# Two small products of a linear attention laid out in halves and quarters of the matrix array

## The chip, the cores and the metric

The kernel runs on one core of a Trainium2 chip. The metric is the device time of one execution in microseconds (us), less is better. The core has a matrix engine (PE, with PEld for its weight loads), a vector engine (DVE), a scalar engine (ACT), GpSimd (POOL), a queue of transfers on SyncE (SP), and DMA engines. PE reads its operands from the on-chip memory and writes into accumulation banks (PSUM), which DVE and ACT empty.

## The reference

Linear attention over 4 batches of 8 heads with 576 rows of 64, then two feed-forward blocks over all 2304 rows (model width 512, inner width 1536). All is float32.

```python
q_s = softmax(q, axis=-1)            # over the 64 features of a row
k_s = softmax(k, axis=2)             # over the 576 rows
kv  = einsum('bhsd,bhse->bhde', k_s, v)      # 64 x 64 for each head
x   = einsum('bhsd,bhde->bhse', q_s, kv)     # then heads side by side: 2304 x 512
x   = (silu(x @ w_gate) * (x @ w_val)) @ moe_w_out
out = ((x @ w_a) * (x @ w_b)) @ moe2_w_out
```

## The kernel before

**Tiles.** The attention is worked in 16 units: 4 batches (b) by 4 pairs of heads (g). A unit holds two heads side by side in the 128 columns or partitions (HG = 2, D = 64), and its 576 rows as four slices of 128 (R = 4) and a rest of 64. The names in a unit are `kx`, `kb` (turned maxima of k, and their spread over the partitions), `kv` (k^T v of both heads), `ks` (sums and reciprocals), `kvbd` (a 128 by 128 matrix with the two scaled 64 by 64 blocks on its diagonal, zero elsewhere), `qt` and `ql` (q turned, main part and rest), `xt` and `xl` (x turned, main part and rest). Buffers of the first two batches are called `ut`; those of the third and fourth `ua`, `uc` and `uq`.

**k^T v (lines 726 to 750).** Five products per unit add up in one PSUM tile of 128 by 130: weights are 128 columns of k (two heads), the moving operand is 130 columns of v (two heads of 64, each with a column of ones that gives the sum of k). The result also holds the two products of one head's k with the other head's v; they are left unread. DVE or ACT scales the two wanted 64 by 64 blocks into `kvbd`.

**x (lines 790 to 800).** One product per unit with `kvbd` as weights and 512 moving columns. For the first batch the result goes straight into the on-chip operand `xhl` of the first feed-forward block. For the other three batches ACT copies it to the buffer `xs` and issues one transfer of 256 KB to a buffer in device memory, from which a later block reads it.

**Feed-forward blocks.** Every float32 weight is converted into a high and a low part by a chain of ACT, DVE and POOL instructions (`convert`, lines 404 to 441), and each product is three reduced-precision products of these parts. The first feed-forward block runs over the batches 0 and 1 as f = 0 to 11 (`u` at line 857, `acc` at line 884); the other work of that block and the second one uses sub-products `p`, `q`, `o` (lines 1136, 1220, 1247 to 1257). The units of batch 1 stand among the products of batch 0 in the first block, those of batches 2 and 3 among those of batch 1.

**What sets the order.** Every instruction is an entry of a plan (`add`), with an engine, an assumed cost, what it reads and writes, and a due time that is worked out backwards or given. `Plan.order` simulates the engines with these costs and picks, per engine, the ready entry that is due first; entries with a second engine (`other`) go where they would end earlier; PSUM banks are given out in the same pass. `Plan.search` repeats that 160 times, shifts a few due times at random each time, and keeps the shortest plan. The instructions are then written out in that order, and each engine runs its own list strictly in that order; an instruction waits until its operands and its buffer are there. So the assumed costs and the seed of the random shifts (line 220) set the order of all engines.

Of the kernel before, what the change touches and what calls it, by code (L numbers as in the profile page):

```python
# [9 lines left out]
F32 = mybir.dt.float32  # L10
# [21 lines left out]
class Plan:  # L32
# [184 lines left out]
    def search(self):  # L217

        self.prepare()
        rng, best = random.Random(0), None  # L220
        for n in range(self.ROUNDS):
            kept = self.due
            if best:
                self.due = [d + rng.uniform(-3, 3) if rng.random() < 0.03 else d for d in kept]
            try:
                found = self.order()
            except RuntimeError:
                self.due = kept
# [16 lines left out]
def kernel(  # L245
# [24 lines left out]
    nc = tc.nc  # L270
# [78 lines left out]
    WHOLE = ("a0", "xraw")  # L349
    AHEAD = 3  # L350
    TOP = 122880.0
    LEAST = 2.0 ** -15

    NP = NF // 2
# [171 lines left out]
    def attend(b, g, xhl, due):  # L526
# [30 lines left out]
        def kx():  # L557
            return col(A, a0, m).rearrange("p (r e) -> p r e", r=R)
# [16 lines left out]
        def vx():  # L575
            return vg()[:, 0:G, :].rearrange("p (h r) d -> p h r d", h=HG)
# [18 lines left out]
        def small(shape, tag):  # L595
            return Buf(hp, shape, F32, (tag + "0", tag + "1"), f"{tag}{u}")

        def psum(shape, name, tag=None):
            if b == 0 and tag:
                return Buf(pg, shape, F32, (tag,), f"{name}{u}")  # L600
            return Buf(pg, shape, F32, AT_BANKS[b], f"{name}{u}")
# [121 lines left out]
            row(ql, m, G, [*QRL, (st, "maxl")], QL)  # L723


        pk, ks = psum([P, HG, D1], "kv"), small([P, 2, HG], "ks")

        def kv():
            for r in range(R):
                nc.tensor.matmul(pk(), lhsT=kx()[:, r, :], rhs=vx()[:, :, r, :], start=(r == 0), stop=False)  # L730
            nc.tensor.matmul(pk(), lhsT=kl(), rhs=vg()[:, G:G + 1, :].to_broadcast([P, HG, D1]),
                             start=False, stop=True)

        add("tensor", 1.3, kv, [K_, KL, *VS, VL, (C, "ones")], [pk])
        add("vector", 0.16, lambda: nc.vector.tensor_scalar(
            out=ks()[:, 0, :], in0=pk()[:, :, D], scalar1=EPS, scalar2=None, op0=ALU.add), [pk], [ks])
        add("vector", 0.16, lambda: nc.vector.reciprocal(out=ks()[:, 1, :], in_=ks()[:, 0, :]), [ks], [ks])
        for h in range(HG):
            o = rest_cols(h)

            def scale(h=h, o=o):
                nc.vector.tensor_scalar(out=kvbd()[o, o], in0=pk()[o, h, 0:D], scalar1=ks()[o, 1, h:h + 1],
                                        scalar2=None, op0=ALU.mult)

            def scale_too(h=h, o=o):
                nc.scalar.mul(out=kvbd()[o, o], in_=pk()[o, h, 0:D], mul=ks()[o, 1, h:h + 1])
# [33 lines left out]
        def turn_rest():  # L780
# [6 lines left out]
        add("scalar", act_us(SL), lambda: nc.scalar.copy(out=qT()[:, SM:S], in_=pl()), [pl], [QTL])  # L787


        px, py = psum([P, SM], "xt", f"acc{g}"), Buf(pg, [P, SL], F32, AT_BANKS[max(b, 1)], f"xl{u}")  # L790
        add("tensor", 0.95, lambda: nc.tensor.matmul(  # L791
            px(), lhsT=kvbd(), rhs=qT()[:, 0:SM], start=True, stop=True), [QT, *BDS], [px], due=due)
        if xhl is not None:
            split(lambda: xhl()[:, 0, g, :], lambda: xhl()[:, 1, g, :], px, SM,
                  (xhl, (0, g)), (xhl, (1, g)), px, psum=True)
# [233 lines left out]
    def parts(s):  # L1029
# [6 lines left out]
        for q, (t, h) in enumerate(((0, 0), (0, 1), (1, 0), (1, 1))):  # L1036
            i = blocks[t]
            pieces = [(i, 0, width, 0)] if i < B else [(i - 1, width, SM - width, 0), (i, 0, B * SL, SM - width)]
            for src, at, size, to in pieces:
                last_x[:] = [dma(lambda q=q, h=h, src=src, at=at, size=size, to=to: nc.sync.dma_start(  # L1040
                    out=RAW[q][1]().rearrange("p (c n) -> p c n", c=2)[:, :, to:to + size],
                    in_=xd[l][src]()[:, 2 * h:2 * h + 2, at:at + size]),
                    P * 2 * size * 4, [(xd[l][src], (2 * h + c, 0)) for c in range(2)] if s == 0 else [xd[l][src]],
                    [(RAW[q][0][0], (RAW[q][0][1], to))], after=[*last_x, *(() if s or t == 0 else pair_buf["after"])])]

        def keys(q):
# [328 lines left out]
```

## Time and profile before

| | us |
|---|---|
| median of 3 runs (lowest, highest) | 946.86 (946.19, 947.77) |
| the profiled execution, its own time | 947.02 |
| its span in the trace | 945.2 |
| PE busy | 913.9 (97%) |
| DVE busy | 641.7 (68%) |
| ACT busy | 519.2 (55%) |

The profile comes from one execution. A busy time of PE contains the way through the array of each product, which overlaps with the next product; so products that stand back to back show a longer duration than the distance of their starts. In the chain of waits a step counts only the time until the next step begins, which is the time that the product really takes from the span. A float32 product appears as two passes, each with its own weight load (x2 for one product).

### The profile page before, as it was taken

To read this page: it belongs to the slowest core of one execution; us is meant where nothing else is said; L and a number is where in the kernel's file an instruction comes from. 1 tells how busy PE (TensorE), PEld (TensorE's weight loads), DVE (VectorE), ACT (ScalarE), POOL (GpSimd) and SP (SyncE) were. 2 spreads that over 40 slices of the span, in tenths; PEclk is the share of its full clock that TensorE was granted. 3 is DMA by queue.
4 is the path that set the end of the run, shared out by engine and by line. 5 is a ranking of instruction groups with operands and counts; after the bars stand their busy time and mean duration, and the time that the engine had idled before them with its cause. 6 is when DMAs were issued, how large, how long until landed. Compare 5 with 4: busy or idle time off the path is not lost.

```text
span 945.2 us, 12797 instructions
## 1 busy us (share of the span) xinstructions
PE 913.9 (97%) x4400; PEld 755.7 (80%) x4400; DVE 641.7 (68%) x1025; ACT 519.2 (55%) x1020; POOL 331.9 (35%) x323
## 2 busy tenths in 40 slices
PE   5699999999999999999999999999999999999998
PEld 4477777788887888888888888888888888888886
DVE  6899996544376887877778665775786444564444
ACT  4798876878675665455464456443644453333310
POOL 6534221112053322434455542432565113342210
PEclk9889999999999999999999999999999999999999
DMA  9858765464327545355322653422213210110003
GB/s 263 271 199 267 233 230 190 121 191 131 90 89 233 156 143 153 123 163 156 112 90 71 214 174 121 133 89 89 68 50 123 86 45 23 45 45 23 23 1 112
DMA packets 108153, 121.43 MB, mean 128 GB/s; under 512 B 31928, under 2 KB 83896, under 8 KB 107960
## 3 DMA queue, kind: packets, MB, share of 16 engines
q1 hardware_dynamic: 102424, 116.55, 39.8%
q10 hardware_dynamic: 5664, 4.07, 1.4%
q8 instruction: 35, 0.57, 0.3%
q14 instruction: 30, 0.25, 0.1%
HBM read 88.60 MB, written 31.98 MB: 128 GB/s over the span
## 4 chain that ended last, share of the span: by engine, by line
PE 80%; DVE 8%; DMA 6%; ACT 3%; issue 2%; SPq 1%; POOL 0%; DVEq 0%; ACTq 0%
PE p L1136 34%; PE o L1247 15%; PE u L857 9%; PE q L1220 7%; PE o L1249 6%; PE acc L884 5%; PE o L1257 2%; DVE l2w L324 1%; PE kv L730 1%; DMA wr<-in_moe_w_gate_dram 1%; PE xt L791 1%; DVE sums L324 1%; DMA wr<-in_moe_w_out_dram 1%; DMA wf<-a 1%; DMA raww<-wf 1%
## 5 line engine op out<-in xcount | busy, mean ns | idle before, releaser
L1136 PE MATMUL p<-l2w,l2w 128*128 128x512 f32 x1512 | 353.1, 390 | 1.3 <-DVE temps L324 1.1
L1136 PEld LDWEIGHTS p<-l2w,l2w 128*128 128x128 f32 x1512 | 283.1, 188 | 61.7 <-DVE temps L324 2.4
L857 PE MATMUL u<-xhl,w 128*128 128x512 f32 x552 | 143.9, 408 | 5.0 <-DVE w L324 4.7
L331 ACT CAST l2w<-raww 128x512 fp32r<-128x512 f32 x144 | 88.1, 621 | 79.7 <-PE p L1136 39.9
L324 POOL TENSOR_TENSOR l2w<-raww,l2w 128x512 fp32r<-128x512 f32 x68 | 97.0, 1431 | 97.9 <-ACT l2w L331 97.8
L857 PEld LDWEIGHTS u<-xhl,w 128*128 128x128 f32 x552 | 102.2, 192 | 31.8 <-DVE w L324 6.8
L324 DVE TENSOR_TENSOR sums<-o,sums 128x512 f32<-128x512 f32 x120 | 82.4, 689 | 53.4 <-PE o L1247 39.9
L324 DVE TENSOR_TENSOR temps<-p,temps 128x512 f32<-128x512 f32 x90 | 62.1, 690 | 66.4 <-PE p L1136 65.2
L1247 PE MATMUL o<-l2w,hp 128*128 128x512 f32 x288 | 82.3, 394 | 0.3 <-DVE sums L324 0.2
L1148 ACT COPY temps<-p 128x512 f32<-128x512 f32 x72 | 42.4, 588 | 68.3 <-PE p L1136 68.2
L324 DVE TENSOR_TENSOR l2w<-raww,l2w 128x512 fp32r<-128x512 f32 x76 | 55.6, 742 | 26.6 <-ACT l2w L331 26.5
L884 PE MATMUL acc<-h,w 128*128 128x512 f32 x288 | 73.6, 399 | 0.0
L1220 PE MATMUL q<-rest,l2w 128*128 128x256 f32 x432 | 65.4, 283 | 0.0
L1247 PEld LDWEIGHTS o<-l2w,hp 128*128 128x128 f32 x288 | 53.4, 188 | 12.9 <-DVE sums L324 1.8
L884 PEld LDWEIGHTS acc<-h,w 128*128 128x128 f32 x288 | 52.9, 188 | 11.9
L1220 PEld LDWEIGHTS q<-rest,l2w 128*128 128x128 f32 x432 | 58.6, 192 | 0.9
L1247 PE MATMUL o<-l2w 128*128 128x512 f32 x192 | 54.5, 392 | 0.0
L496 POOL TENSOR_TENSOR latewr<-latewr 128x512 uint32<-128x512 uint32 x17 | 23.9, 1410 | 63.5 <-DVE latewr L491 47.9
L1247 PE MATMUL o<-l2w,l2w 128*128 128x512 f32 x168 | 44.6, 390 | 0.0
L324 POOL TENSOR_TENSOR raww<-raww,spare 128x512 f32<-128x512 f32 x15 | 20.1, 1339 | 69.2 <-DVE l2w L324 63.8
L1249 PE MATMUL o<-hp,l2w 128*128 128x512 f32 x144 | 41.9, 399 | 1.6 <-DVE sums L324 1.6
L1247 PEld LDWEIGHTS o<-l2w 128*128 128x128 f32 x192 | 36.0, 188 | 8.2
(197 smaller groups left out, 1483.5 us busy)
## 6 DMA issues: line engine op xcount, KB each, us to landing
raww<-wf SPq DMA_DIRECT2D x36, 512.0 KB, 4.2
raww<-wf SPq DMA_DIRECT2D x36, 256.0 KB, 3.6
wf<-latewr SPq DMA_DIRECT2D x36, 256.0 KB, 3.4
wf<-a SPq DMA_DIRECT2D x16, 384.0 KB, 2.8
latewr<-in_moe_w_a_dram SPq DMA_DIRECT2D x24, 256.0 KB, 3.0
latewr<-in_moe_w_b_dram SPq DMA_DIRECT2D x24, 256.0 KB, 3.6
latewr<-in_moe_w_out_dram SPq DMA_DIRECT2D x12, 512.0 KB, 5.0
wr<-in_moe_w_gate_dram SPq DMA_DIRECT2D x22, 256.0 KB, 3.1
```

Source lines behind the costliest of these rows:

```text
L324: engine.tensor_tensor(out=out(), in0=x(), in1=y(), op=op)
L331: add("scalar", act_us(n), lambda: nc.scalar.copy(out=hi(), in_=src()), src_keys, [hi_key])
L496: engine.tensor_tensor(out=u32(), in0=u32(), in1=r()[..., 0], op=ALU.add)
L730: nc.tensor.matmul(pk(), lhsT=kx()[:, r, :], rhs=vx()[:, :, r, :], start=(r == 0), stop=False)
L857: nc.tensor.matmul(ps()[:, 0:n], lhsT=wv[:, c, :], rhs=x()[:, xs, c, 0:n], start=(a == 0 and c == 0), stop=(a == 2 and c == KD - 1))
L884: nc.tensor.matmul(ps()[:, 0:n], lhsT=w()[:, 4 + ws, o * P:(o + 1) * P], rhs=h()[:, hs, 0:n], start=begin, stop=end)
L1136: nc.tensor.matmul(ps()[:, 0:width], lhsT=wv(o)[:, m, ws, c, :], rhs=ops_x[o][xs][1]().rearrange("p (c n) -> p c n", c=2)[:, c, 0:width], ...
L1148: add("scalar", act_us(n), lambda: nc.scalar.copy(out=to[1]()[:, 0:n], in_=ps()[:, 0:n]), [ps], [to[0]], due=main["at"] + main["soon"])
L1220: nc.tensor.matmul(ps[m]()[:, 0:256], lhsT=wv(o)[:, m, ws, c % 2, :], rhs=rest_x[xs][1]().rearrange("p (c n) -> p c n", c=KD)[:, c, :], st ...
L1247: nc.tensor.matmul(ps(), lhsT=lhs(i, hs), rhs=outs_w[i][1]()[:, ws * 512:(ws + 1) * 512], **ends)
L1249: nc.tensor.matmul(ps()[:, 0:width], lhsT=outs_w[i][1]()[:, ws * 512 + r * P:ws * 512 + (r + 1) * P], rhs=hs2[i][t][1]()[:, hs * 512:hs * ...
L1257: nc.tensor.matmul(ps()[:, o * 256:(o + 1) * 256], lhsT=outs_w[i][1]()[:, ws * 512 + at:ws * 512 + at + P], rhs=rest_h[1]()[:, (2 * i + hs ...
```

## The change

The change does four things. k^T v of a unit is ten products of 64 by 65 instead of five of 128 by 130: for each slice of rows first head 0, with its 64 weight columns in the left column half of the array (`tile_position=(0, 0)`, results in the PSUM partitions 0 to 63), then head 1 in the right half (`(0, 64)`, partitions 64 to 127). The products of one head with the other head's v are no longer computed. x of batches 1 to 3 is four products of 64 by 64 weights with 256 moving columns each, in the four quarters of the array (`tile_position=(h * D, t * D)`, head h and half t of the columns); the two of one head go into one PSUM tile, the second head into another; ACT makes two copies of 256 columns, and issues two transfers of 128 KB. Batch 0 keeps its single product. The plan's assumed costs become 0.8 for k^T v (1.3 before) and 0.27 for each pair of products of x (0.95 before for the one product), and the seed becomes 2.

```diff
-        rng, best = random.Random(0), None
+        rng, best = random.Random(2), None
...
+    XT = 0.27
+    KV = 0.8
...
-        pk, ks = psum([P, HG, D1], "kv"), small([P, 2, HG], "ks")
+        pk, ks = psum([P, D1], "kv"), small([P, 2], "ks")
 
         def kv():
-            for r in range(R):
-                nc.tensor.matmul(pk(), lhsT=kx()[:, r, :], rhs=vx()[:, :, r, :], start=(r == 0), stop=False)
-            nc.tensor.matmul(pk(), lhsT=kl(), rhs=vg()[:, G:G + 1, :].to_broadcast([P, HG, D1]),
-                             start=False, stop=True)
-
-        add("tensor", 1.3, kv, [K_, KL, *VS, VL, (C, "ones")], [pk])
+            for r in range(R + 1):
+                for h in range(HG):
+                    lhs, rhs = (kx()[:, r, rest_cols(h)], vx()[:, h, r, :]) if r < R else (kl()[:, rest_cols(h)], vg()[:, G, :])
+                    nc.tensor.matmul(pk()[rest(h), :], lhsT=lhs, rhs=rhs, start=r == 0, stop=r == R,
+                                     tile_position=(0, h * D))
+
+        add("tensor", KV, kv, [K_, KL, *VS, VL, (C, "ones")], [pk])
...
-        px, py = psum([P, SM], "xt", f"acc{g}"), Buf(pg, [P, SL], F32, AT_BANKS[max(b, 1)], f"xl{u}")
-        add("tensor", 0.95, lambda: nc.tensor.matmul(
-            px(), lhsT=kvbd(), rhs=qT()[:, 0:SM], start=True, stop=True), [QT, *BDS], [px], due=due)
...
-            ob = Buf(op, [P, 512], F32, ("ob0", "ob1"), f"xs{u}")
-            add("scalar", act_us(SM), lambda: nc.scalar.copy(out=ob(), in_=px()), [px], [ob])
-            dma(lambda: nc.scalar.dma_start(out=xd[0][b]()[:, g, :], in_=ob()), P * SM * 4,
-                [ob], [(xd[0][b], (g, 0))], queue="scalar")
+            ob, half = Buf(op, [P, 512], F32, ("ob0", "ob1"), f"xs{u}"), SM // 2
+            for h in range(HG):
+                ph = psum([P, half], f"xt{h}_")
+
+                def run(h=h, ph=ph):
+                    for t in range(2):
+                        nc.tensor.matmul(ph()[t * D:(t + 1) * D, :], lhsT=kvbd()[rest_cols(h), rest_cols(h)],
+                                         rhs=qT()[rest_cols(h), t * half:(t + 1) * half], start=True, stop=True,
+                                         tile_position=(h * D, t * D))
+
+                add("tensor", XT, run, [QT, *BDS], [ph], due=due)
+                add("scalar", act_us(half), lambda h=h, ph=ph: nc.scalar.copy(
+                    out=ob()[:, h * half:(h + 1) * half], in_=ph()), [ph], [(ob, h)])
+            for t in range(2):
+                dma(lambda t=t: nc.scalar.dma_start(
+                    out=xd[0][b]()[:, g, t * half:(t + 1) * half].rearrange("(h e) n -> e h n", h=HG),
+                    in_=ob()[t * D:(t + 1) * D, :].rearrange("e (h n) -> e h n", h=HG)), P * SM * 2,
+                    [ob], [(xd[0][b], (g, t))], queue="scalar")
```

The new costs and the new seed move instructions on every engine. Line numbers of the changed kernel are 2 to 18 higher: 734 is k^T v (730 and 731 before), 807 is x of the later batches (791 before), 875 and 902 are `u` and `acc` (857 and 884 before).

On PE, at the second unit of batch 2, among the products of the first feed-forward block; before:

```order
L884 MATMUL acc_1_1727<-h_1_0_1675,w_0_329 128x512 x3
L730 MATMUL kv_1741<-uc_1549,ua_1557 128x130 x4
L731 MATMUL kv_1741<-uc_1549,ua_1557 128x130
L884 MATMUL acc_2_1755<-h_1_0_1675,w_0_329 128x512 x3
L667 MATMUL kx_1764<-ident,km_1736 128x128
L884 MATMUL acc_3_1767<-h_1_0_1675,w_0_329 128x512 x3
L778 MATMUL qt_1774<-ident,ua_1557 128x128 x4
L857 MATMUL u_1_2_0_1780<-xhl_1_1507,w_2_568 128x512 x4
L781 MATMUL ql_1789<-ident_84,ua_1557 128x64
L857 MATMUL u_1_2_0_1780<-xhl_1_1507,w_2_568 128x512 x4
L791 MATMUL xt_1799<-uc_1549 128x512
```

The same unit in the changed kernel:

```order
L781 MATMUL qt_1823<-ident,ua_1633 128x128 x4
L902 MATMUL acc_3_1829<-h_1_0_1753,w_0_391 128x512 x3
L875 MATMUL u_1_2_0_1835<-xhl_1_1587,w_2_582 128x512 x4
L734 MATMUL kv_1844<-uc_1622,ua_1633 64x65 x10
L784 MATMUL ql_1858<-ident_84,ua_1633 128x64
L875 MATMUL u_1_2_0_1835<-xhl_1_1587,w_2_582 128x512 x8
L669 MATMUL kx_1880<-ident,km_1775 128x128
L807 MATMUL xt_9_1882<-uc_1622 64x256 x2
L875 MATMUL u_1_2_1_1888<-xhl_1_1587,w_2_582 128x512 x4
L807 MATMUL xt_9_1896<-uc_1622 64x256 x2
```

The ten small products of k^T v stand together; the four of x stand as two pairs, here with a full-array product between them. In 5 of the last 9 units both pairs stand together, in 4 they are parted as here.

On DVE, up to the end of the conversion of the weights f = 1 (`w_1`; `tm`, `st`, `kr` with `ut` are steps of the first unit of batch 1); before:

```order
L431 ISA a_1_0_396<-wr_1_199,a_1_0_396 128x3072
L417 TENSOR_SCALAR a_0_2_428<-a_0_2_428 128x512
L324 TENSOR_TENSOR tm_452<-ut_391 128x2x2x64
L420 TENSOR_SCALAR a_0_2_428<-a_0_2_428 128x512
L689 TENSOR_REDUCE st_459<-ut_391 128x8
L426 SCALAR_TENSOR_TENSOR a_0_2_428<-wr_0_2_191,a_0_2_428 128x512
L871 TENSOR_TENSOR u_0_0_1_401<-s_0_0_446,u_0_0_1_401 128x512
L670 TENSOR_REDUCE kr_475<-kx_456 128x1
L692 TENSOR_REDUCE st_459<-ut_391 128x1
L324 TENSOR_TENSOR w_1_463<-a_1_0_396,w_1_463 128x2x3x256
```

The same place in the changed kernel:

```order
L433 ISA a_1_0_436<-wr_1_199,a_1_0_436 128x3072
L422 TENSOR_SCALAR a_0_2_457<-a_0_2_457 128x512
L889 TENSOR_TENSOR u_0_0_1_418<-s_0_0_454,u_0_0_1_418 128x512
L428 SCALAR_TENSOR_TENSOR a_0_2_457<-wr_0_2_191,a_0_2_457 128x512
L324 TENSOR_TENSOR w_1_476<-a_1_0_436,w_1_476 128x2x3x256
L324 TENSOR_TENSOR h_0_0_483<-u_0_0_1_418,h_0_0_483 128x512
L691 TENSOR_REDUCE st_504<-ut_413 128x8
L324 TENSOR_TENSOR tm_507<-ut_413 128x2x2x64
L694 TENSOR_REDUCE st_504<-ut_413 128x1
```

The four steps of the attention unit that stood ahead of `w_1` now stand behind it (`kr` further on than these rows). On ACT the changed order has 34 table loads (the switch between the functions Exp and Silu) instead of 32.

## Rows read from the trace of the kernel before

**Rows 1.** The page: busy times, and busy tenths and granted clock in 40 slices.
```profile
PE 913.9 (97%) x4400; PEld 755.7 (80%) x4400; DVE 641.7 (68%) x1025; ACT 519.2 (55%) x1020; POOL 331.9 (35%) x323
...
PE   5699999999999999999999999999999999999998
...
DVE  6899996544376887877778665775786444564444
...
PEclk9889999999999999999999999999999999999999
```

**Rows 2.** Stretches: length, then busy PE, PEld, DVE, ACT, POOL, clock, DMA.
```profile
40.00:60.00 20.00, 15.55 (x62) 12.12 (x61) 20.00 (x28) 17.60 (x34) 6.08 (x10) 0.83 0.73 231
...
80.00:100.00 20.00, 18.99 (x92) 15.07 (x91) 19.03 (x34) 18.01 (x41) 8.63 (x12) 1.00 0.86 267
...
120.00:140.00 20.00, 19.21 (x91) 15.43 (x90) 18.46 (x25) 15.29 (x23) 4.49 (x4) 1.00 0.71 236
140.00:160.00 20.00, 19.78 (x91) 15.47 (x90) 14.59 (x24) 9.99 (x17) 1.16 (x6) 1.00 0.67 221
160.00:180.00 20.00, 19.74 (x96) 15.67 (x95) 12.82 (x31) 19.36 (x56) 6.93 (x18) 1.00 0.36 113
180.00:200.00 20.00, 20.00 (x105) 16.06 (x104) 9.49 (x28) 14.35 (x50) 2.45 (x10) 1.00 0.60 174
```

**Rows 3.** PE's waits, whole span, then 120 to 260 us: us, times, longest.
```profile
PE u L857 <- DVE w L324: 4.7, 4, 1.9
...
PE xt L791 <- ACT ut L785: 0.8, 1, 0.8
```

**Rows 4.** The chain of waits, 178 to 200 us: start, length, step.
```profile
180.53 0.89 PE kv L730 x8
181.43 0.22 PE kv L731 x2
...
185.67 0.86 PE xt L791 x2
...
188.48 0.17 PE xl L801 x2
```

**Rows 5.** Line 730: ns least/median/most, first and last start.
```profile
L730 PE MATMUL kv<-ut x64: 273/273/557, 14.9 to 141.6; 128*128 128x130 f32 x64
...
L730 PE MATMUL kv<-uc,ua x64: 272/273/277, 168.9 to 250.4; 128*128 128x130 f32 x64
```

**Rows 6.** DVE in order of time around weights f = 1: start, us, instruction.
```profile
43.08 0.42 DVE L324 TENSOR_TENSOR tm<-ut 128x256 f32<-128x256 f32 x1
...
43.75 0.68 DVE L689 TENSOR_REDUCE st<-ut 128x8 f32<-128x512 f32 x1
...
45.55 0.55 DVE L670 TENSOR_REDUCE kr<-kx 128x1 f32<-128x384 f32 x1
46.01 0.28 DVE L692 TENSOR_REDUCE st<-ut 128x1 f32<-128x128 f32 x1
46.21 1.86 DVE L324 TENSOR_TENSOR w<-a,w 128x1536 fp32r<-128x1536 f32 x1
```

**Rows 7.** PE in order of time there; in brackets its idle time before.
```profile
48.12 8.31 PE L857 MATMUL u<-xhl,w 128*128 128x512 f32 x24 [1.58 <-DVE w L324]
```

**Rows 8.** ACT's groups, 160 to 260 us: busy us, mean ns.
```profile
L868 ACT ACT_TABLE_LOAD x9 | 11.5, 1283 | 0.4 <-ACT uc L787 0.3
...
L798 ACT COPY xs<-xt 128x512 f32<-128x512 f32 x8 | 4.7, 591 | 2.1 <-PE xt L791 2.1
...
L805 ACT COPY xq<-xl 128x64 f32<-128x64 f32 x8 | 1.6, 203 | 0.0
```

**Rows 9.** Line 799, ACT's issue of x's transfer: ns least/median/most.
```profile
L799 ACTq DMA_DIRECT2D x<-xs x12: 326/327/392, 76.9 to 255.4; - x12
```

More of the change, by code (lines that the diff above doesn't have):

```diff
@@ L723, in attend @@
             row(ql, m, G, [*QRL, (st, "maxl")], QL)
-        pk, ks = psum([P, HG, D1], "kv"), small([P, 2, HG], "ks")
+        pk, ks = psum([P, D1], "kv"), small([P, 2], "ks")
         def kv():
-            for r in range(R):
-                nc.tensor.matmul(pk(), lhsT=kx()[:, r, :], rhs=vx()[:, :, r, :], start=(r == 0), stop=False)
-            nc.tensor.matmul(pk(), lhsT=kl(), rhs=vg()[:, G:G + 1, :].to_broadcast([P, HG, D1]),
-                             start=False, stop=True)
-        add("tensor", 1.3, kv, [K_, KL, *VS, VL, (C, "ones")], [pk])
+            for r in range(R + 1):
[4 more added lines that the diff above has]
+        add("tensor", KV, kv, [K_, KL, *VS, VL, (C, "ones")], [pk])
         add("vector", 0.16, lambda: nc.vector.tensor_scalar(
-            out=ks()[:, 0, :], in0=pk()[:, :, D], scalar1=EPS, scalar2=None, op0=ALU.add), [pk], [ks])
-        add("vector", 0.16, lambda: nc.vector.reciprocal(out=ks()[:, 1, :], in_=ks()[:, 0, :]), [ks], [ks])
+            out=ks()[:, 0:1], in0=pk()[:, D:D1], scalar1=EPS, scalar2=None, op0=ALU.add), [pk], [ks])
+        add("vector", 0.16, lambda: nc.vector.reciprocal(out=ks()[:, 1:2], in_=ks()[:, 0:1]), [ks], [ks])
         for h in range(HG):
@@ L741, in scale @@
             def scale(h=h, o=o):
-                nc.vector.tensor_scalar(out=kvbd()[o, o], in0=pk()[o, h, 0:D], scalar1=ks()[o, 1, h:h + 1],
+                nc.vector.tensor_scalar(out=kvbd()[o, o], in0=pk()[o, 0:D], scalar1=ks()[o, 1:2],
                                         scalar2=None, op0=ALU.mult)
             def scale_too(h=h, o=o):
-                nc.scalar.mul(out=kvbd()[o, o], in_=pk()[o, h, 0:D], mul=ks()[o, 1, h:h + 1])
+                nc.scalar.mul(out=kvbd()[o, o], in_=pk()[o, 0:D], mul=ks()[o, 1:2])
             add("vector", 0.29, scale, [pk, ks, BD], [(C, f"kvbd{h}")],
@@ L787, in attend @@
         add("scalar", act_us(SL), lambda: nc.scalar.copy(out=qT()[:, SM:S], in_=pl()), [pl], [QTL])
-        px, py = psum([P, SM], "xt", f"acc{g}"), Buf(pg, [P, SL], F32, AT_BANKS[max(b, 1)], f"xl{u}")
-        add("tensor", 0.95, lambda: nc.tensor.matmul(
-            px(), lhsT=kvbd(), rhs=qT()[:, 0:SM], start=True, stop=True), [QT, *BDS], [px], due=due)
+        py = Buf(pg, [P, SL], F32, AT_BANKS[max(b, 1)], f"xl{u}")
         if xhl is not None:
+            px = psum([P, SM], "xt", f"acc{g}")
+            add("tensor", 0.95, lambda: nc.tensor.matmul(
+                px(), lhsT=kvbd(), rhs=qT()[:, 0:SM], start=True, stop=True), [QT, *BDS], [px], due=due)
             split(lambda: xhl()[:, 0, g, :], lambda: xhl()[:, 1, g, :], px, SM,
@@ L1042, in parts @@
                     in_=xd[l][src]()[:, 2 * h:2 * h + 2, at:at + size]),
-                    P * 2 * size * 4, [(xd[l][src], (2 * h + c, 0)) for c in range(2)] if s == 0 else [xd[l][src]],
+                    P * 2 * size * 4, [(xd[l][src], (2 * h + c, t)) for c in range(2) for t in range(2)] if s == 0 else [xd[l][src]],
                     [(RAW[q][0][0], (RAW[q][0][1], to))], after=[*last_x, *(() if s or t == 0 else pair_buf["after"])])]
```

## The prediction

> **What bounds the kernel now.** I read the page first. PE is busy for 97% of the span, and from the fourth of the 40 slices on it shows 9 in nearly all; DVE is at 9 from slice 2 to slice 6 and then falls [rows 1]. So there are two stages, and the stretches part them. From 40 to 140 us DVE is busy for 18.5 to 20 of 20 us: the first weights are being converted, and PE's stalls on `u` that a DVE conversion ended, 4.7 us in all, belong to it [rows 2, 3]. From 140 us on DVE falls to 14.6 and then 9.5 of 20, while PE stands at 19.7 to 20 [rows 2]. From 120 to 260 us the longest single wait of PE is 0.8 us, once [rows 3]. There a microsecond less of PE work is a microsecond off the end, if the other engines keep up; before that it mostly turns into more waiting for weights.
>
> Last I read the chain of waits in the saturated stretch, because it prices a PE step by what it takes from the span: k^T v of a unit is 0.89 + 0.22 = 1.11 us (ten passes of 0.111), x is 0.86 us (two passes of 0.43), and a product with only 64 moving columns 0.17 us (two passes of 0.085) [rows 4]. The busy duration of a k^T v pass is 273 ns [rows 5]; the difference to 111 ns is the way through the array, which the next pass covers.
>
> **Which units count.** The passes of the third and fourth batch start between 168.9 and 250.4 us, 64 at line 730, eight per unit: eight units, all in the saturated stage. The last unit of the second batch starts at 141.6 us and belongs there too [rows 5]. That makes nine. The other three units of batch 1 stand in the stage bound by conversion, the four of batch 0 in the start, where the first products wait for weights afterwards anyway; I count those seven at nothing. If that cover is thinner than I think, they are worth up to 2 us.
>
> **k^T v.** A unit had ten passes of 130 columns and gets twenty of 65 columns, on alternating column halves. The trace of before has no product in a part of the array, so I bound it. Best: the two halves always run side by side, ten times half of 0.111, which is 0.56 us. Worst: they run one behind the other, each at the 0.085 us of a 64-column pass [rows 4], 1.70 us. If the pairs run side by side but no pair beats that short pass, it is ten times 0.085, or 0.85. The short pass loads 128 weight columns, the new ones load 64, so I take the middle of 0.56 and 0.85, 0.70 us. It saves 0.41 per unit and 3.7 us over nine.
>
> **x of the later batches.** Two passes of 512 columns (0.43 each) become eight of 256 columns, 0.215 each by the same rate. Best: all four quarters run together, two rounds, 0.43 us. Two at a time it is 0.86, what it was. Worst: one behind the other, 1.72. Where the two pairs stand together (5 of the nine units in the changed order) I take four at a time, where another product parts them (4 of nine) two at a time: 5 x 0.43 = 2.15 us saved.
>
> **Switching.** Nine groups of k^T v and 5 + 8 groups of x change the shape in which the array is used, once in and once out, 44 times. No row of before shows such a switch. At best it costs nothing; at worst each time the array must run empty, 0.273 - 0.111 = 0.162 us [rows 4, 5], which is 7.1 us. The nearest row is the 64-column product `xl`, which stands between products of another operand type and width and costs 0.17 us with both changes in it [rows 4]; by it I take nothing, and keep the rest as a rival. The Trainium skill speaks against my choice: its page "TensorEngine Tiling (Array Packing)", section "Tiling Modes", says that changing the tiling mode drains the engine. By that rule the sum below would end 7.1 us higher; no run here shows it yet.
>
> **What the new order does to the start.** The four DVE steps of the first unit of batch 1 that now stand behind the weights f = 1 took, from start to next start, 0.34 + 0.60 + 0.46 + 0.20 = 1.6 us [rows 6], and PE had sat idle for 1.58 us just before its product with those weights [rows 7]. I take 1.6 us saved. The same regrouping goes on for later weights, so it could be 4 us; it could also be a loss. ACT gets more: per unit a copy of 512 columns (0.591) becomes two of 256, about 0.39 each by a line through the 64-column copy (0.203) [rows 8], and a second issue of 0.33 us [rows 9], together 0.5 us for 12 units; and two more table loads of 1.28 us [rows 8]. Cover: ACT is busy for 15 to 18 of 20 us up to 140, so there is room for the 2 us of the units of batch 1 and the table loads, though not everywhere; between 160 and 180 us it is at 19.4 [rows 2], where a unit or two would show, 0.5 to 1 us. If all of it lay on the path in the start it would cost 4.5 us.
>
> The second PSUM tile of x uses the two banks that the units of these batches already share. Each is held for a copy of about 0.39 us and PE has products of the feed-forward block between the steps, so I count nothing. The two transfers carry the same bytes to a buffer that is read long after.
>
> **The sum.** It is made against the profiled execution, 947.02 us, whose span is 945.2 us; the median of the runs shown is 946.86, 0.02% less. 947.0 - 3.7 - 2.15 - 1.6 = 939.6 us. The best ends together (0.55 and 0.43 in all nine, 4 in the start, 2 in the covered units) would give 932.
>
> **The rivals.**
> *Passes begin strictly in order.* A float32 product is a high and a low pass on the same quarter (x2 in [rows 4]), which cannot run together; if a pass may not begin before its forerunner in the list has begun, only the low pass of one product overlaps with the high pass of the next. Then x is five rounds of 0.215 where the four stand together (+0.22) and twice three where they are parted (+0.43): + 2.8 us over nine units. k^T v hardly suffers, eleven rounds for ten, say 0.75: - 3.2. 947.0 + 2.8 - 3.2 - 1.6 = 945.0 us, range 942 to 948. For it speaks that the list has the passes in just that order; against it, that the trace of before cannot show overlap of this kind at all. The Trainium skill bears on it: "TensorE: Matmul & The Clock Gate", in the section on packing small matmuls, says that products start and end in program order.
> *Switching drains the array.* The gain on PE stays, and 7.1 us are paid for it: 939.6 + 7.1 = 946.7 us, range 943 to 949.
> *The parts don't run together.* This is the one that ends slower. Every pass takes its own time behind the one before: x 1.72 instead of 0.86 on nine units, + 7.7; k^T v between 1.11 and 1.70, say 1.40, + 2.6. 947.0 + 10.3 - 1.6 = 955.7 us, range 952 to 961. It decides as soon as two half-width passes together take more than 0.111 us, or four quarter passes more than 0.43. It is also how the change would not do what it says.
> *The new order of the start loses.* The PE gain is as forecast, but ACT's extra work falls in front of weights that PE waits for: 947.0 - 5.85 + 4 = 945.2 us, range 943 to 948. For it: ACT at 17.6 and 18.0 of 20 between 40 and 100 us [rows 2]. Against it: DVE is fuller there, and its list got shorter ahead of f = 1.
>
> **Chances and range.** Forecast 0.42 (its own range 932 to 943), strict order 0.20, draining 0.14, parts one by one 0.14, a worse start 0.10. What a measurement of this kernel can tell from no change is about 0.2%, 1.9 us: faster is under 945.0, slower over 948.8. Faster: 0.41 of the forecast, half of strict order, 0.04 of draining, 0.04 of the worse start, 0.59. Slower: 0.14 from parts one by one and 0.03 from the tails, 0.17. The rest, 0.24, is no change. The range of 932 to 952 leaves out most of parts one by one and little else.
>
> **What would show it.** In the profile after, the chain's step for k^T v of a unit should be near 0.70 us (over 1.1: parts one by one), the two steps of x together near 0.43 to 0.6 where they stand together (near 1.08: strict order). An idle of about 0.16 us of PE or a long first pass at each change of shape would show draining. Idle of PE before the first product of f = 1 should be gone; if PE waits for weights longer than 4.7 us in all up to 140 us, the start is worse. The prediction is wrong if PE's steps are as forecast but a wait for ACT or DVE stands in the chain after 140 us.

## The result, and the profile after

The changed kernel takes 959.21 us (median of 4 runs, 957.20 to 959.98) against 946.84 us in the same comparison; the ratio is 1.0119, 95% interval 1.0105 to 1.0133 (the quotient of the two medians, 1.0131, lies in it). It is slower by about 12 us where 7 us less were forecast, and outside the range. The profiled execution has a span of 957.9 us (945.2 before).

The page of the changed kernel, the lines that answer to [rows 1]:

```profile
PE 917.5 (96%) x4632; PEld 747.0 (78%) x4632; DVE 647.5 (68%) x1031; ACT 521.7 (54%) x1035; POOL 324.0 (34%) x316
...
PE   5679899999999999999999999999999999999998
...
DVE  6888888645468777777787667766687543564444
...
PEclk9889999999999999999999999999999999999999
```

PE is 3.6 us busier although every k^T v got shorter, and DVE's full slices are 8s where 9s stood: in the stage that DVE bounds, DVE is less busy than before. The stretches show it more sharply; columns as in [rows 2]:

```profile
40.00:60.00 20.00, 11.31 (x40) 8.40 (x40) 16.17 (x20) 14.47 (x30) 4.32 (x2) 0.83 0.66 209
...
140.00:160.00 20.00, 18.72 (x102) 13.70 (x101) 18.92 (x30) 11.56 (x18) 2.59 (x6) 1.00 0.58 178
```

Between 40 and 60 us DVE works 16.2 of 20 us (20.0 before); between 140 and 160 us, where it had been down to 14.6, it still works 18.9: the conversion of the weights ends later. PE's waits say the same, over the whole span (us in total, times, longest):

```profile
PE u L875 <- DVE w L324: 12.7, 4, 6.0
```

That row had 4.7 us [rows 3]. Taking 36 to 180 us as one stretch, before and then after:

```profile
36.00:180.00 144.00, 134.38 (x602) 106.69 (x603) 126.53 (x196) 117.38 (x244) 42.19 (x67) 0.96 0.66 211
```

```profile
36.00:180.00 144.00, 126.90 (x638) 96.12 (x637) 121.86 (x187) 113.58 (x226) 37.58 (x54) 0.94 0.67 209
```

PE is idle for 17.1 us instead of 9.6, and the mean granted clock is 0.94 instead of 0.96, which is up to 2.9 us more of full speed (a low clock costs nothing while PE stands idle). From the first `u` of the first feed-forward block (at 33.0 us before, 33.5 after) to the last `acc` of its part over batch 0 it takes 7.9 us longer (131.0 before, 138.8 after). The wait ahead of the weights f = 1, which was to vanish [rows 7], has grown:

```profile
45.76 7.62 PE L875 MATMUL u<-xhl,w 128*128 128x512 f32 x24 [5.97 <-DVE w L324]
```

The saturated stage gave nothing back either: from that `acc` to the tenth `u` over batch 1 it takes 99.1 us, where it took 97.6. The chain of waits of the changed kernel there, the rows that answer to [rows 4]:

```profile
194.93 0.58 PE xt L807 x4
195.51 1.14 PE u L875 x4
196.65 0.58 PE xt L807 x4
```

A pair of quarters takes 0.58 us until the next product begins; four were to take 0.43. The step of k^T v is seen in the chain of the kernel that has only that half of the change (experiment 4):

```profile
200.64 0.73 PE kv L734 x20
```

0.73 us where 0.70 was forecast and 1.11 stood before. Last, the shapes themselves, line and operation, ns least/median/most, which answer to [rows 5]:

```profile
L734 PE MATMUL kv<-uc,ua x160: 218/222/272, 176.8 to 263.9; 128*64 128x65 f32 x160
...
L807 PE MATMUL xt<-uc x64: 375/402/428, 181.7 to 267.0; 64*64 64x256 f32 x64
```

In the trace the two heads' passes of k^T v begin 4 to 8 ns apart, in all pairs but one. At 244.31 us, where four quarters of x stand together, the four high passes begin within 21 ns, and 266 ns later the four low passes within 21 ns. So the parts do run side by side.

One more row moved: ACT's issue of x's transfers, of which there are now two a unit. It answers to [rows 9]:

```profile
L815 ACTq DMA_DIRECT2D x<-xs x24: 582/610/637, 83.0 to 268.7; - x24
```

An issue takes 0.61 us, where the forecast took over the 0.33 us of before.

### The profile page after: what moved, and what is told of

Same layout as the page of the kernel before. It is cut to its first block, busy times and chain, and to the rows that moved or that the text cites. A ratio compares the mean times of both kernels' runs of the same rounds, so it can differ in the third digit from the quotient of the medians.

```text
span 957.9 us, 13276 instructions
## 1 busy us (share of the span) xinstructions
PE 917.5 (96%) x4632; PEld 747.0 (78%) x4632; DVE 647.5 (68%) x1031; ACT 521.7 (54%) x1035; POOL 324.0 (34%) x316
## 4 chain that ended last, share of the span: by engine, by line
PE 81%; DVE 7%; DMA 5%; ACT 4%; issue 2%; POOL 1%; SPq 0%; ACTq 0%; DVEq 0%; POOLq 0%
PE p L1154 36%; PE o L1265 15%; PE u L875 8%; PE q L1238 7%; PE o L1267 6%; PE acc L902 4%; PE o L1275 2%; DVE l2w L324 2%; DMA wf<-a 1%; PE xt L807 1%; ACT w L438 1%; PE kv L734 1%; ACT ut L717 1%; DMA x<-xs 1%; PE qt L781 1%
## 5 line engine op out<-in xcount | busy, mean ns | idle before, releaser
L875 PE MATMUL u<-xhl,w 128*128 128x512 f32 x552 | 147.8, 413 | 13.6 <-DVE w L324 12.7
L331 ACT CAST l2w<-raww 128x512 fp32r<-128x512 f32 x144 | 88.1, 621 | 69.0 <-PE p L1154 32.7
L324 DVE TENSOR_TENSOR l2w<-raww,l2w 128x512 fp32r<-128x512 f32 x76 | 56.3, 754 | 34.4 <-ACT l2w L331 34.1
L902 PE MATMUL acc<-h,w 128*128 128x512 f32 x288 | 76.1, 409 | 2.0 <-ACT h L331 2.0
L1238 PEld LDWEIGHTS q<-rest,l2w 128*128 128x128 f32 x432 | 58.6, 192 | 0.9
L331 ACT CAST l2w<-temps 128x512 fp32r<-128x512 f32 x36 | 22.3, 621 | 43.9 <-PE o L1265 28.9
L324 POOL TENSOR_TENSOR raww<-raww,spare 128x512 f32<-128x512 f32 x13 | 17.8, 1366 | 82.4 <-DVE l2w L324 77.7
L498 POOL TENSOR_TENSOR latewr<-latewr 128x512 uint32<-128x512 uint32 x17 | 23.4, 1376 | 61.1 <-DVE latewr L493 47.6
```

The lines of the kernel that those rows point to most:

```text
L324: engine.tensor_tensor(out=out(), in0=x(), in1=y(), op=op)
L331: add("scalar", act_us(n), lambda: nc.scalar.copy(out=hi(), in_=src()), src_keys, [hi_key])
L498: engine.tensor_tensor(out=u32(), in0=u32(), in1=r()[..., 0], op=ALU.add)
L875: nc.tensor.matmul(ps()[:, 0:n], lhsT=wv[:, c, :], rhs=x()[:, xs, c, 0:n], start=(a == 0 and c == 0), stop=(a == 2 and c == KD - 1))
L902: nc.tensor.matmul(ps()[:, 0:n], lhsT=w()[:, 4 + ws, o * P:(o + 1) * P], rhs=h()[:, hs, 0:n], start=begin, stop=end)
L1238: nc.tensor.matmul(ps[m]()[:, 0:256], lhsT=wv(o)[:, m, ws, c % 2, :], rhs=rest_x[xs][1]().rearrange("p (c n) -> p c n", c=KD)[:, c, :], st ...
```

## The experiments

All ratios are against the kernel before on the same chip in the same job (its medians there: 947.80, 947.60 and 947.45 us), with their 95% interval.

**1. k^T v in halves, the order untouched.** All engines' lists stay those of before; only the products of k^T v differ, and the shapes of the small steps that read them.

```diff
-            for r in range(R):
-                nc.tensor.matmul(pk(), lhsT=kx()[:, r, :], rhs=vx()[:, :, r, :], start=(r == 0), stop=False)
...
+            for r, h in [(r, h) for r in range(R + 1) for h in range(HG)]:
...
+                nc.tensor.matmul(pk()[rest(h), :], lhsT=lhs, rhs=rhs, start=r == 0, stop=r == R,
+                                 tile_position=(0, h * D))
```

> The kernel before with the new k^T v alone: ten products in column halves, the assumed cost (1.3) and the seed (0) left as they were, so that every engine's list is that of before. In the trace of the changed kernel the step of k^T v in the chain of waits fell from 1.11 to 0.73 us, and about 0.10 us is lost on the way in and up to 0.15 us on the way out. Theory A (the products are faster, switching eats a part, and the loss of 12.4 us is the new order of all engines): 9 units in the saturated stage x 0.28 us less, 944.5 us (942 to 946.5). Theory B (the products in parts of the array cost the time, by themselves or by what they do to the clock): 949 us or more.

Measured: 947.65 us, ratio 0.9998 (0.9989 to 1.0006). No gain can be told, and the time lies between the ranges of the two theories. The trace shows a saving and where it may go. From the last `acc` over batch 0 to the tenth `u` over batch 1, the stage takes 96.4 us instead of 97.6. Earlier, though, the first `u` begins at 34.4 us instead of 33.0, and PE then waits longer for weights, 2.08 us at 106 us where it had been 1.89 us, and the granted clock, which had stayed at 1.00 there, falls in the stretch behind it. The stretch from 100 to 120 us of this kernel; the same stretch of before reads 18.11 (x84) and clock 1.00:

```profile
100.00:120.00 20.00, 17.92 (x88) 13.99 (x87) 19.18 (x32) 17.07 (x37) 1.64 (x3) 0.91 0.73 236
```

The whole runs say the same of the clock: its mean is 0.991 over the 11 runs of this kernel and 0.994 over the 19 of the kernel before.

**2. The halves for batches 1 to 3 only,** again on the lists of before (batch 0 keeps the whole array).

```diff
+            for r, h in [(r, h) for r in range(R + 1 if b else 0) for h in range(HG)]:
```

> The kernel before with k^T v in column halves for batches 1 to 3 alone; batch 0 keeps the whole array, x too, and every engine's list is that of before. Theory C: the 1.35 to 1.8 us that the halves of batch 0 cost in the start (the clock rises at 24.0 us instead of 19.5) are gone, and 0.2 us per unit stay: 945.5 us, 0.9980 to 0.9990 of before. Rival E (the start of that run was late for another reason, or k^T v in halves delays later work as well): 0.9995 to 1.001 of before.

Measured: 947.72 us, ratio 0.9996 (0.9981 to 1.0011). The interval holds both the expectation and no change. The same stretch falls to a clock of 0.83 after a wait of 2.85 us. That the halves of the first batch harm the start is not supported; experiment 4, which has them too, begins its first `u` at 31.67 us, and experiment 3, which has none, at 31.66.

**3. The new lists alone.** The order of the changed kernel on every engine, its two copies and two issues too, but the products of k^T v and x on the whole array.

```diff
-                        nc.tensor.matmul(ph()[t * D:(t + 1) * D, :], lhsT=kvbd()[rest_cols(h), rest_cols(h)],
-                                         rhs=qT()[rest_cols(h), t * half:(t + 1) * half], start=True, stop=True,
-                                         tile_position=(h * D, t * D))
+                    nc.tensor.matmul(ph(), lhsT=kvbd(), rhs=qT()[:, h * half:(h + 1) * half], start=True, stop=True)
```

> The changed kernel's plan, costs and seed, so that every engine's list is that of the changed kernel, but with products on the whole array: k^T v as five products of 128 by 130, each pair of products of x as one product of 128 weight columns and 256 moving columns. Theory A (the order lost the time): 957 to 963 us, about 1.5 us over the changed kernel, since the tiled products save only 9 x 0.28 us on k^T v and lose about 1.2 us on x over the nine units. Theory B (the tiled products cost the time): 945 to 949 us.

Measured: 954.10 us, ratio 1.0061 (1.0047 to 1.0075). That lies between the ranges of the two theories: half of the loss is there without a single product in a part of the array. PE's wait for `w` is 12.7 us here as well. Two things come along. The lists hold ACT's added copies and issues, so these and the mere order are not told apart. And x's transfers leave from all 128 partitions again, where the quarters need another form; an issue of them takes 0.33 us instead of 0.61:

```profile
L811 ACTq DMA_DIRECT2D x<-xs x24: 326/327/635, 81.1 to 265.9; - x24
```

**4 and 5. One half of the change on the new lists:** k^T v in halves with x whole, then x in quarters with k^T v whole.

> Every engine's list as in the changed kernel; k^T v in column halves as there, x on the whole array. Theory C: 8.80 - 7.25 = 1.6 us less over the eight units of batches 2 and 3, but about 2 us more in the start, where k^T v in halves goes with a clock that rises later: 954.5 us (953 to 956). Rival D: 957 or more.

> Every engine's list as in the changed kernel; x of the later batches in quarters as there, k^T v on the whole array. With the whole array for both this list took 954.1 us, with both in parts 959.2. Theory C (switching): a group of products in parts costs about 0.10 us on the way in and 0.11 on the way out; x of a unit costs 0.80 us where its pairs stand together and 2 x 0.79 where they are parted, against 0.87 on the whole array. Eight units of batches 2 and 3: 9.73 - 6.95 = + 2.8 us, so 956.9 (955.5 to 958.5). Rival D (x in parts is as good as free, and k^T v in parts is what costs): 953 to 955.

Measured: 951.38 us, ratio 1.0039 (1.0028 to 1.0050), and 957.25 us, ratio 1.0107 (1.0086 to 1.0128). The first lies below its range (953 to 956): the 2 us that the halves were to cost in the start did not come. The second lies in its range. Each taken against the kernel before of its own job, the lists alone are at +6.3 us, with the halves at +3.8, with the quarters at +9.7: the halves give 2.5 us (the two intervals just overlap), and the quarters, with the transfers that they need, cost 3.3.

**6 to 8. The seed and the assumed costs.** The kernel before with seed 2; the change with seed 0; the change with the costs that the trace shows.

```diff
-        rng, best = random.Random(0), None
+        rng, best = random.Random(2), None
...
-    XT = 0.27
-    KV = 0.8
+    XT = 0.79
+    KV = 0.92
```

> The kernel before with nothing changed but the seed of the plan's random shifts, 2 instead of 0. Theory A (the order decides, and the order of before is a lucky one of its kind): 950 to 962 us. If all seeds are alike and only the new costs make a bad order: 945 to 949 us. Theory B says nothing of it, but under B the order should not matter much: 945 to 949 us.

> The changed kernel with seed 0 instead of 2, all else as in the changed kernel. Theory A: another order, so a time that differs from 959.2 by several us, 945 to 963, with the steps of k^T v and x in the chain as they are. Theory B (tiled products): 957 to 961 us.

> The changed kernel with the plan's assumed costs set to what the trace shows, 0.92 for k^T v (0.8) and 0.79 for each pair of products of x (0.27). If the plan's order is bad because it counts on products that are too cheap (theory F): 948 to 953 us. If the new order is worse for its extra copies, issues and table loads on ACT and by chance (theory G): 955 to 963 us.

Measured: 950.55 us, ratio 1.0031 (1.0018 to 1.0045); 959.26 us, 1.0122 (1.0105 to 1.0139); 957.37 us, 1.0110 (1.0090 to 1.0129). The seed moves the old kernel by 2.7 us; but seed 0 doesn't mend the change, whose time stays the same although its order is another, and truer costs bring it down by 2 or 3 us at most. So the one other order that was run with the old kernel's own instructions is slower than that of before; in the other two kernels the time is that of the order and of the products in parts together.

**9. One instruction of the new order moved back.** In the trace of the changed kernel ACT's longest wait in the conversion stage is for a load. In order of time, start, us, instruction, and in brackets the idle time before it and what ended it:

```profile
43.82 0.58 ACT L331 CAST h<-u 128x512 fp32r<-128x512 f32 x1
48.78 0.90 ACT L417 ACTIVATE wr<-wr 128x768 uint32<-128x768 uint32 x1 [4.38 <-DMA wr<-in_moe_w_out_dram]
49.58 1.57 ACT L412 ACTIVATE a<-wr 128x1536 f32<-128x1536 f32 x1
```

DVE in the same stretch, up to the next weights' step that needs ACT's `a`:

```profile
47.15 0.28 DVE L694 TENSOR_REDUCE st<-ut 128x1 f32<-128x128 f32 x1
51.19 0.96 DVE L419 TENSOR_SCALAR a<-a 128x1536 f32<-128x1536 f32 x1 [3.76 <-ACT a L412]
```

The instruction that waits scales a half of the weights f = 4, whose loads were issued only at 42.5 to 43.5 us; the absolute value of f = 2 is queued behind it, and DVE behind that. In the kernel before, ACT makes that scaling at 61.4 us, after the absolute value and the cast of f = 2. On the lists of experiment 3 it is put behind the cast of f = 2; all other rows stay:

```diff
+        moved, behind = self.marks["low", 0, 4], self.marks["cast", 0, 2]
+        done.remove(moved)
+        done.insert(done.index(behind) + 1, moved)
```

> The changed kernel's lists with the products on the whole array (954.10 us, ratio 1.0061), and of these lists one instruction moved: ScalarE's scaling of the low words of the weights f=4, first half, stands behind the conversion of f=2 instead of ahead of f=2's and f=3's absolute values. Theory (that scaling waits 4.4 us for a load, and VectorE's conversion of f=2 and f=3 is queued behind it): VectorE's wait of 3.8 us is gone, TensorE's waits for converted weights fall from 12.7 us by about 3.5, time about 950.6 us, ratio 1.0026. Rival (the conversions as a whole bound that stage, or the wait is hidden): within 0.5 us of 954.1, ratio 1.0056 to 1.0066.

Measured: 951.88 us, ratio 1.0045 (1.0033 to 1.0057), about 2 us less than experiment 3, beside 3.5 expected; the two intervals overlap. DVE's wait fell:

```profile
DVE a L424 <- ACT a L416: 1.1, 1, 1.1
```

It did not fall to nothing, because the absolute value of f = 2 was not ready either. ACT now waits for a step of POOL on `a`:

```profile
ACT a L416 <- POOL a L438: 2.5, 1, 2.5
```

So f = 2 gained 2.5 us, not 3.8: its product begins at 58.6 us, in experiment 3 at 61.1. PE's row did not fall by 3.5; it rose a little, because PE now reaches the same waits earlier:

```profile
PE u L876 <- DVE w L328: 13.3, 4, 6.6
```

What fell is the total: PE's idle time between 36 and 180 us is 15.2 us (16.4 in experiment 3), and the mean clock 0.95 instead of 0.93. The expectation looked at one row where it should have looked at the stretch. Experiment 3, then this one:

```profile
36.00:180.00 144.00, 127.57 (x569) 101.64 (x569) 122.78 (x187) 113.59 (x229) 35.10 (x49) 0.93 0.65 207
```

```profile
36.00:180.00 144.00, 128.82 (x582) 102.48 (x581) 124.58 (x193) 116.15 (x242) 35.02 (x50) 0.95 0.66 211
```

At the last `acc` over batch 0 this profile is 3.6 us ahead of that of experiment 3, and 1.5 us of it are lost again at 599 us, where PE waits for `temps` as it does not in experiment 3.

**10. The same instruction moved the other way, in the kernel before:** ahead of the absolute value of f = 2, as the change has it; nothing else.

```diff
+        moved, ahead = self.marks[0, 4][1], self.marks[0, 2][0]
...
+        done.remove(moved)
+        done.insert(done.index(ahead), moved)
```

> The kernel before, with the same scaling of f=4's first half moved the other way, ahead of the absolute value of f=2, as the changed kernel has it; nothing else is moved. Theory: ScalarE stands from 46.5 us to the landing of that load (issued at 43.7, so about 48.5) and takes 0.9 us itself; f=2 and f=3 come up to 3 us later on VectorE: 947 to 950 us, ratio 1.001 to 1.003. Rival (VectorE's conversions as a whole bound that stage): ratio 1.000.

Measured: 952.07 us, ratio 1.0052 (1.0034 to 1.0070): more than the 3 us expected. ACT's wait and DVE's:

```profile
ACT wr L420 <- DMA wr<-in_moe_w_out_dram: 2.6, 1, 2.6
```

```profile
DVE a L423 <- ACT a L415: 2.5, 1, 2.5
```

One ACT instruction of 0.9 us, moved ahead of 29 others in a list of 1020, makes the old kernel 0.5% slower. How it does so is less clear. PE's wait for `w` did not grow (4.7 us before); the attention's steps wait longer for ACT, `ql` 2.2 us (0.8 before) and `kv` 1.6 us (none over 0.3 before):

```profile
PE u L863 <- DVE w L329: 4.6, 4, 1.9
...
PE ql L787 <- ACT ut L791: 2.2, 1, 2.2
...
PE kv L736 <- ACT ut L714: 1.6, 1, 1.6
```

And the profiled execution took 956.26 us, 4 us more than the median; its clock is lower already up to 36 us, 0.91 against 0.95 before, ahead of the edit.

**11. The parted pairs joined.** In the changed kernel, the first pair of x's quarters is moved down PE's list to stand directly ahead of the second, in four of the five units where they are parted (in the fifth the plan's buffers don't allow it). No other engine's list changes.

```diff
+        for x0, c0, x1, c1 in self.marks["pairs"]:
+            down, up = list(done), list(done)
+            for n, m in ((x0, x1), (c0, c1)):
+                down.remove(n)
+                down.insert(down.index(m), n)
...
+            if gap:
+                done = down if not clash(down) else up if not clash(up) else done
```

> The changed kernel (959.2 us), with the first pair of x's quarters moved down to stand directly ahead of the second in four of the five units where they are parted; every other engine's list stays as it is. Theory (a parted pair costs a second switching and its own time, 1.58 us a unit parted against 0.80 together): 0.78 us less in each of the four, of which three stand where TensorE never waits: 2.3 to 3.1 us less, 956.1 to 956.9 us, ratio 1.0098 to 1.0106. Rival (switching is free, x's quarters lose for another reason): within 0.5 us of 959.2, ratio 1.012 to 1.013.

Measured: 954.64 us, ratio 1.0076 (1.0064 to 1.0088), 4.6 us less than the change and more than the 2.3 to 3.1 expected. The step itself can be read in three kernels at the same place of PE's list, the second unit of batch 2. The changed kernel:

```profile
207.62 1.17 PE L875 MATMUL u<-xhl,w 128*128 128x512 f32 x4
208.72 0.65 PE L807 MATMUL xt<-uc 64*64 64x256 f32 x4
209.30 1.20 PE L875 MATMUL u<-xhl,w 128*128 128x512 f32 x4
210.42 0.65 PE L807 MATMUL xt<-uc 64*64 64x256 f32 x4
211.00 3.07 PE L902 MATMUL acc<-h,w 128*128 128x512 f32 x12
```

The same lists with whole products (experiment 3):

```profile
206.09 1.17 PE L870 MATMUL u<-xhl,w 128*128 128x512 f32 x4
207.09 0.59 PE L805 MATMUL xt<-uc 128*128 128x256 f32 x2
207.33 1.28 PE L870 MATMUL u<-xhl,w 128*128 128x512 f32 x4
208.46 0.59 PE L805 MATMUL xt<-uc 128*128 128x256 f32 x2
208.70 3.14 PE L897 MATMUL acc<-h,w 128*128 128x512 f32 x12
```

The pairs joined:

```profile
204.19 2.07 PE L897 MATMUL u<-xhl,w 128*128 128x512 f32 x8
206.20 0.66 PE L828 MATMUL xt<-uc 64*64 64x256 f32 x8
206.79 3.06 PE L924 MATMUL acc<-h,w 128*128 128x512 f32 x12
```

From the first start of `u` to the start of `acc`, the same eight `u` and one x take 3.38 us parted, 2.61 whole, 2.60 joined. Eight passes in four quarters take as long as four in two, 0.59 and 0.58; parting them costs 0.78 us. Three such units of the saturated stage were joined, 2.3 us; PE's stretch from the last `acc` over batch 0 to the tenth `u` over batch 1 got only 1.3 us shorter (99.1 to 97.8). Of the rest of the 4.6 us, 1.8 lie ahead of the first `u` at 32 to 33 us, where nothing was edited: up to 36 us the mean granted clock was 0.95 in the profile of the change, 1.00 in this one and 0.95 again in experiment 12, which has the same products there. So this part belongs to the execution and not to the edit.

The rows of the weight loads (PEld) show one thing that the switch takes away. With whole products the weights of x are loaded 0.22 us ahead of the product, beneath the one before (experiment 3):

```profile
206.87 0.41 PEld L805 LDWEIGHTS xt<-uc 128*128 128x128 f32 x2
207.09 0.59 PE L805 MATMUL xt<-uc 128*128 128x256 f32 x2
```

In quarters the load begins only with the product itself (the change):

```profile
208.71 0.20 PEld L807 LDWEIGHTS xt<-uc 64*64 64x64 f32 x4 [0.37 <-issue]
208.72 0.65 PE L807 MATMUL xt<-uc 64*64 64x256 f32 x4
```

**12. Both edits in the changed kernel.**

> The changed kernel with both edits: the scaling of f=4 moved back on ScalarE, and the pairs joined in four units. If both theories hold and their gains add: 959.2 - 3.5 - 2.3 to 3.1 = 952.6 to 953.4 us, ratio 1.0061 to 1.0069. If only one holds: 955.7 to 956.9. If neither: 959.

Measured: 954.10 us, ratio 1.0069 (1.0056 to 1.0081), in none of the ranges. The scaling gives 0.5 us more here, not 3.5, and the intervals don't tell 0.5 us from nothing. PE's wait for `w` is still 12.6 us. So that instruction is one slip of the new order, and not its only one; which others hold the weights up was not taken apart. ACT's table loads are one suspect: between 97 and 118 us it makes four in experiment 9 and two in the kernel before, at 1.28 us each. That was not tried.

## Why the prediction failed

**The start, minus 1.6 us: wrong, and the largest error.** The step failed where it said "Cover: ACT is busy for 15 to 18 of 20 us up to 140, so there is room". I had compared DVE's ten rows around `w_1`, found four steps gone from ahead of it, and f = 1 did come sooner: its product begins at 45.8 us instead of 48.1 [rows 7]. But busy time says nothing about where in a list an instruction stands. One ACT instruction, ahead of its data, held up f = 2 and the later weights by some 2.5 us (experiment 9). The lists alone cost 6.3 us (experiment 3), where the bounds were -4 and +4.5. A single row is worth some 2 us of it in experiment 9 and 4.6 us the other way in experiment 10; the rest is the order of other rows or ACT's added work, not broken down.

**ACT's added work: sized at half.** The forecast has "a second issue of 0.33 us" and 0.5 us a unit in all. Two issues of 0.61 us and two copies of 0.37 make 1.05 us more than before, 12.6 us for 12 units. How much of that lay on the path no run separates.

**Switching at nothing: wrong.** It was the choice "The nearest row is the 64-column product `xl`". That row stands between full-array products; it shows a change of operand, not of tiles. The price can be worked out now. Two halves side by side would stream k^T v of a unit in 0.56 us, ten times half of 0.111, and what it takes between full-array products is 0.93 us, 0.09 to 0.11 of it ahead of the first pass and as much behind the last step of 0.73; for x it is 0.43 streaming and 0.79 in all, one pair or two. Each group pays 0.36 us, a little more than the 2 x 0.162 that was taken as the worst; 22 groups make 7.9 us. The Trainium skill's rule, "TensorEngine Tiling (Array Packing)", "Tiling Modes", that a change of mode drains the engine, agrees with these traces, about 0.10 us at either end of a group. The weights, too, are not loaded ahead across the change (experiment 11); which of the two sets the price no run separates.

**k^T v at 0.70: right in the step, wrong in the worth.** 0.73 was measured. But 0.41 a unit was not the gain, because 0.2 us stand outside the step: 1.12 us to 0.93. Over the eight units of batches 2 and 3 that is 1.6 us, not 3.3.

**x: the mechanism half right, the sign wrong.** Four quarters do run together, so what was said of the joined pairs ("I take four at a time") holds. "Two at a time it is 0.86, what it was", used for the parted pairs, does not: each parted pair pays for its own switch, 1.58 us a unit. By the measured prices x saves 0.07 us in each of the four joined units of these batches and loses 0.72 in each of the four parted ones, 2.6 us in all; the trace has 9.7 us of x there, against 6.9 before, and experiment 5 stands 3.3 above experiment 3, transfers included.

**Nine units that count: right, but the others were not harmless.** In the start the saved time turned into longer waits for weights, as forecast; that such a wait may be followed by a lower clock was not forecast (experiments 1 and 2).

**The rivals.** *Strict order of passes* is refuted: x would have stepped by 1.08 us where four stand together, and the four high passes run at once. The Trainium skill's sentence on program order ("TensorE: Matmul & The Clock Gate", "Packing small matmuls") holds for whole products here, whose quarters begin about 7 ns apart and end in that order. The passes of different products interleave, all high ones first; in what order the engine's list has them no run shows. *Parts one by one* is refuted too, and that the time fell into its range is luck: k^T v would have stepped by 1.1 to 1.7 us. *Switching drains* had a nearly right price for a group, and its sum for PE, -5.85 + 7.1 = +1.3 us, is near the 3.3 - 2.5 = +0.8 of experiments 4 and 5; it came to 946.7 us because it kept the start's 1.6 us as a gain. *A worse start* had the right place, with 4 us where 6.3 came. None held two of these together, and the truth is both: order +6.3, quarters with their switching +3.3, halves with theirs -2.5, which makes 7.1.

**What stays open.** These parts make 7 of the 12 us. The profiles, one of each kernel (that of experiment 5 took 960.13 us, 2.9 above its median), tell where the rest lies. The stretches of the span in us, cut at the first `u`, at the last `acc` over batch 0, at the tenth `u` over batch 1 and at the first `p`:

| | before | lists (3) | with halves (4) | with quarters (5) | the change |
|---|---|---|---|---|---|
| up to the first `u` | 33.0 | 31.7 | 31.7 | 32.7 | 33.5 |
| first block, batch 0 | 131.0 | 139.7 | 137.7 | 140.9 | 138.8 |
| batch 1, up to the tenth `u` | 97.6 | 97.5 | 95.6 | 100.2 | 99.1 |
| batch 1, the rest | 27.6 | 28.8 | 28.8 | 29.6 | 31.9 |
| all behind it | 656.1 | 654.6 | 654.6 | 654.8 | 654.6 |

The lists lose in batch 0, where the weights are converted. In the third row the halves give 1.9 us and the quarters cost 2.7, near the 1.6 and 2.6 of their prices. What doesn't add up in the change is 1.8 us ahead of the first `u`, where its clock was the lower one (experiment 11), and 3.1 us in the fourth row. There PE waits 2.0 us for ACT's `h`, 0.7 us in experiments 3 and 4 and 1.5 in experiment 5, and behind that wait the granted clock falls, from 296 to 306 us:

```profile
296.00:306.00 10.00, 7.99 (x28) 5.98 (x27) 8.46 (x13) 4.83 (x8) 1.61 (x2) 0.83 0.58 176
```

The passes of `acc` stand 0.43 us apart there instead of 0.23. Experiments 11 and 12 have the same wait of 2.0 us; in 11 the clock falls behind it, to 0.91 from 290 to 310 us, and in 12 it stays at 1.00:

```profile
290.00:310.00 20.00, 17.99 (x78) 14.15 (x77) 15.65 (x20) 9.88 (x17) 5.15 (x4) 1.00 0.72 238
```

So the wait comes with the kernel, and the loss of the clock behind it only in some executions. Over all runs the mean granted clock was 0.988 for the change (4 runs), 0.991 for experiment 3 (4 runs) and 0.994 to 0.995 for the kernel before. Why ACT's `h` comes later with the quarters was not taken apart; their longer issues are a suspect.

## What to carry to other kernels

A product in a part of the array has to save more than the switch into and out of that shape costs, here 0.36 us for each group that stands alone among full-array products; so small tiled products belong next to each other, in one entry of the plan, or nowhere. When a planner reorders everything, reading the rows around the edit is not enough: on each engine's list, look for an instruction that now stands ahead of its data with work queued behind it that others wait for. And to separate a change from the order that it brings, run the new order with the old operations first; here that one run held half of the answer.

## What the runs showed of the hardware

- Full-array products of different operand types change over in under 0.1 us; a change to halves or quarters and back costs 0.36 us, with two quarters in between or four.
- Ahead of a product in quarters the weights were loaded with its start, ahead of the same product on the whole array 0.22 us before it.
- An issue on ACT of a transfer of 128 KB took 0.61 us in the form that the quarters need and 0.33 us from all 128 partitions.
- Float32 products in different quarters run their high passes at the same time; eight passes of 256 columns in four quarters take 0.59 us, four in two 0.58.
- A cheaper product ahead of a wait for weights can make the wait longer, and what follows it can run at a lower clock. Behind the wait at 105 us the mean granted clock from 100 to 120 us was 1.00 in the kernel before (wait 1.89 us), 0.91 in experiment 1 (2.08 us) and 0.83 in experiment 2 (2.85 us): a part of the stretch at 1.2 instead of 2.4 GHz. It does not always come: experiment 4 waited 2.81 us at 114 us, and its clock stayed at 1.00 up to the end of the first block.
